# Splitting the first products of a mixture-of-experts stage, and moving the low halves of its weights behind the last gather

## The chip, the cores and the metric

The kernel runs on one core of one Trainium2 chip. The metric is the device time of the whole kernel in microseconds (us). Three runs of the kernel before took 800.58, 804.08 and 804.29 us; the median is 804.08.

## What is computed

Block-causal attention (64 tokens a block) for 8 batches, 8 heads, 576 tokens and 64 values a head. Its output, seen as 4608 tokens of 512 values, goes through a mixture of 8 experts. Each token goes to one expert, and each expert takes at most 576 tokens: the pairs of token and expert are gone through from the highest logit down, and a pair is taken if the token is still free and the expert not full.

```python
x = attn_out.transpose(0, 2, 1, 3).reshape(4608, 512)
logits = x @ w_gate
for idx in np.argsort(-logits.flatten()):
    tok, e = idx // 8, idx % 8
    if assigned[tok] >= 0 or counts[e] >= 576: continue
    assigned[tok] = e; counts[e] += 1
for e in range(8):
    mask = assigned == e
    out[mask] = np.maximum(x[mask] @ w1[e], 0.0) @ w2[e]   # w1: 512 x 1024, w2: 1024 x 512
```

Inputs and output are 32-bit floats.

## The kernel before

**The two halves of the kernel.** The attention (all lines up to the 500s) fills the first 340 us or so. It writes x to memory with each token as two 16-bit halves side by side: a high half, the value rounded to 16 bits, and a low half, what the rounding lost. The second part is the class `Moe`, and only it is touched.

**Products of halves.** The weights are split in the same way (function `weights`). A product of 32-bit accuracy is then three products of 16-bit numbers, added up in PSUM: high weight by high x, high weight by low x, low weight by high x. In `ffn` they are the list `((0,0),(0,2),(1,0))`, whose first number picks the half of the weight and whose second the half of x. Only the third reads the low half of the weight.

**Order of the work.** Nothing is written out in the order in which it is executed. Each piece of work is a Python generator that yields an engine, a cost in ns and the events that it waits for; a planner (class `Sched`) simulates the engines, always picks the piece that it believes can start first (with priorities), and only then writes its instructions. Each engine executes its own list in that order. The events are the planner's alone: on the chip an instruction waits by semaphores for the data it reads and the buffers it writes. So an event that is added or dropped changes the order of the lists, and the order decides who waits. The engines are named D (VectorE), A (ScalarE), T (TensorE), G (GpSimd, POOL in the profile) and S (SyncE, SP, which issues the plain DMAs).

**The experts one after another.** For the k-th expert in order (which expert that is comes out of the search):

- `route(k)` searches the threshold of the next expert. It begins on VectorE with a maximum over the open logits (L719), a mask (L735) and masked logits (L737), which TensorE transposes (L741). Fourteen rounds follow, in each of which VectorE (L777) and ScalarE (L750) count the logits above three candidates and TensorE adds the counts over partitions (L791, tile `tot`). The number of the expert then goes to `weights(k)`. `invert` turns the mask of chosen tokens into a list of indices; its last steps are the index products on TensorE (L915, tile `ps`) and the cast to integers on VectorE (L918, tile `ix`). L719 of the second search waits in the planner for the low half of the first expert's second row block (`('wc',0,1)`, since `GW=1`), and its transposes (L741) for the third token block (`('xm',0,2)`, `GS=2`).
- `weights(k)` loads the two matrices in eight pieces of 512 KB (SP, L966), four row blocks n = 0 to 3 of w1 and four of w2, into six `raw` buffers. For w1 of the first two experts ScalarE makes the high half with one scaling (L938) and VectorE the low half (L940, raw minus high half). All other pieces are scaled and rounded on ScalarE (L945, L949) and their low half is made on POOL (L951). A `raw` buffer is free again once its low half is made. For the first expert, the loads of w2 are held back by a one-element memset on POOL (L962) that stands behind the last gather.
- `gather(k)` fetches the chosen tokens with five indirect DMAs on POOL (L980), four of 128 tokens and one of 64 (tiles `xg`). For the first two experts `flip` transposes them on TensorE (L990, eight transposes into the PSUM tile `xt`), ScalarE copies one half (L994) and VectorE the other (L995) to the tile `X`. For later experts a DMA transposes (L1005).
- `ffn(k)` makes h (L1030) in PSUM banks shared with y, four in all (tag `g`), from 4 row blocks times 3 products. ScalarE evicts the high half with the relu (L1016, tile `HH`), VectorE the low half (L1018, `HL`). Then y for five token blocks (L1055, and L1059 for the block of 64), whose evictions (L1038, L1042) lead to the scatter on POOL (L1046). h is made in two token slices: for the first expert tokens 0 to 127 and 128 to 575, for the others 0 to 255 and 256 to 575. A slice has eight feature blocks f, taken four at a time.

For the first expert's first slice and first four feature blocks the order of the h products is by row block d: for each d all four f, so that a row block can be used as soon as it is there. Elsewhere it is by f. Both come from these two lines, and the wait in the third is for the event `wc`, set when the low half of row block d has been made:

```python
nf=4 if k==0 and h==0 and f0==0 else 1
for f,d in [(f,d) for a in range(f0,f0+4,nf) for d in range(4) for f in range(a,a+nf)]:
    yield T,3*(w/2.4+3), ... ,('wc',k,d) if k==0 else None
```

The low half of the first expert waits in the planner for its indices:

```python
yield D,1135,('ix',k),('xm',0,0) if k==0 and n in s.XC else None     # XC is empty
```

## Time and profile before

| | |
|---|---|
| median of three runs | 804.08 us (800.58 to 804.29) |
| the profiled execution | 801.86 us |
| its span, from the first to the last instruction | 800.1 us |
| mean granted TensorE clock | 0.965 |
| TensorE (PE) busy | 717.8 us, 90% of the span |
| VectorE (DVE) busy | 585.0 us, 73% |
| ScalarE (ACT) busy | 545.1 us, 68% |
| GpSimd (POOL) busy | 467.0 us, 58% |
| moved by DMA | 121.51 MB, mean 152 GB/s |
| share of PE in the chain that ended last | 58%, DVE 19%, DMA 8%, ACT 8% |

Two pieces of the profile show where the second part of the kernel lies. In the first, the span is cut in 40 slices of 20 us, and each digit is a busy share in tenths. The dip in the middle, slices 18 to 20, is the way from the last attention block through the first search to the first products:

```profile
PE   5889998899999999913898999999999999999995
PEclk9899999999999999955899999999999999999998
```

The other is the list of DMA issues; the columns are target, source, the queue, the count, the size and the median time from issue to landing. The gathers are `xg<-x,ix`:

```profile
xg<-x,ix POOLq DMA_INDIRECT x40, 4.3
out_dram<-yo,ix POOLq DMA_INDIRECT x40, 2.8
```

How the rows further down are read: a row of the timeline has the start (us from the start of the span), the length, the engine, the line of the kernel, the operation, output and inputs (with buffer numbers left out), the shape, and how many instructions it groups; in brackets stands the idle time ahead of it and what ended it. PEclk is the TensorE clock that was granted, as a share of full speed. A length is the time from the start of the first to the end of the last instruction in a row. Matmuls overlap each other in the engine, so a busy TensorE is not TensorE at its peak.

### The profile page before, as it was taken

To read this page: it belongs to the slowest core of one execution; us is meant where nothing else is said; L and a number is where in the kernel's file an instruction comes from. 1 tells how busy PE (TensorE), PEld (TensorE's weight loads), DVE (VectorE), ACT (ScalarE), POOL (GpSimd) and SP (SyncE) were. 2 spreads that over 40 slices of the span, in tenths; PEclk is the share of its full clock that TensorE was granted. 3 is DMA by queue.
4 is the path that set the end of the run, shared out by engine and by line. 5 is a ranking of instruction groups with operands and counts; after the bars stand their busy time and mean duration, and the time that the engine had idled before them with its cause. 6 is when DMAs were issued, how large, how long until landed. Compare 5 with 4: busy or idle time off the path is not lost.

```text
span 800.1 us, 19136 instructions
## 1 busy us (share of the span) xinstructions
PE 717.8 (90%) x6539; PEld 479.6 (60%) x6539; DVE 585.0 (73%) x2395; ACT 545.1 (68%) x1476; POOL 467.0 (58%) x509
## 2 busy tenths in 40 slices
PE   5889998899999999913898999999999999999995
PEld 3666676677767767601644755747557475574752
DVE  6899798988889799488787977969777683730210
ACT  5789888888988888533745859496775947392210
POOL 5788888897889876212324337475471926873001
PEclk9899999999999999955899999999999999999998
DMA  9879999999999991324408049291845819861001
GB/s 203 157 145 179 213 203 209 164 176 204 230 164 222 188 198 35 99 80 133 138 14 294 25 139 231 74 295 42 254 129 184 179 49 273 270 162 40 20 15 45
DMA packets 244305, 121.51 MB, mean 152 GB/s; under 512 B 200816, under 2 KB 227312, under 8 KB 244208
## 3 DMA queue, kind: packets, MB, share of 16 engines
q1 hardware_dynamic: 238320, 101.42, 56.1%
q0 software_dynamic: 5888, 18.88, 7.4%
q8 instruction: 51, 0.84, 0.4%
q14 instruction: 46, 0.38, 0.2%
HBM read 71.32 MB, written 18.87 MB: 113 GB/s over the span
## 4 chain that ended last, share of the span: by engine, by line
PE 58%; DVE 19%; DMA 8%; ACT 8%; issue 3%; POOL 3%; SPq 1%; POOLq 0%; DVEq 0%; ACTq 0%
PE h L1030 23%; PE y L1055 16%; PE psb L463 5%; DVE m L405 5%; PE psb L380 4%; DMA kT<-k 4%; PE psb L498 4%; ACT P L416 4%; DVE kS L350 2%; POOL P L438 2%; PE y L1059 2%; DMA xg<-x,ix 2%; ACT PT L444 2%; DVE jk L776 1%; DMA raw<-in_moe_w_dram 1%
## 5 line engine op out<-in xcount | busy, mean ns | idle before, releaser
L438 POOL TENSOR_TENSOR P<-P,m 128x320 f32<-128x320 f32 (+8 forms) x285 | 209.3, 769 | 48.2 <-DVE m L430 28.4
L1030 PE MATMUL h<-X,W 128*128 128x320 f16 (+3 forms) x1536 | 195.1, 287 | 0.0
L1030 PEld LDWEIGHTS <-W 128*128 128x128 f16 x1536 | 142.2, 98 | 42.7 <-issue 3.1
L416 ACT ACTIVATE P<-psb,m 128x576 f32<-128x576 f32 (+8 forms) x288 | 149.2, 542 | 25.8 <-DVE m L409 19.7
L1055 PE MATMUL y<-W,HH 128*128 128x512 f16 x512 | 152.2, 379 | 0.0
L951 POOL TENSOR_TENSOR W<-raw,W 128x1024 f16<-128x1024 f32 x56 | 118.4, 2136 | 40.6 <-ACT W L949 38.3
L405 DVE TENSOR_REDUCE m<-psb 128x1 f32<-128x576 f32 (+8 forms) x288 | 125.0, 481 | 12.4 <-PE psb L380 11.9
L463 PE MATMUL psb<-mident,P 128*128 128x128 f32 x800 | 106.0, 281 | 10.9 <-POOL P L438 3.6
L1046 POOL DMA_INDIRECT out_dram<-yo,ix x40 | 39.4, 986 | 113.1 <-ACT yo L1038 79.2
L380 PEld LDWEIGHTS <-qT 128*64 128x64 f16 x1408 | 78.1, 112 | 42.8 <-issue 27.8
L380 PE MATMUL psb<-kT,qT 128*64 128x288 f16 (+8 forms) x704 | 91.7, 286 | 10.2 <-ACT P L416 9.7
L463 PEld LDWEIGHTS psb<-mident,P 128*128 128x128 f32 x800 | 87.3, 142 | 22.5 <-POOL P L438 6.4
L498 PE MATMUL psb<-PT,V 128*64 128x448 f32 (+5 forms) x776 | 97.2, 388 | 2.4 <-DVE PT L446 1.9
L980 POOL DMA_INDIRECT xg<-x,ix x40 | 41.6, 1040 | 95.8 <-DVE ix L918 37.7
L1055 PE MATMUL y<-W,HL 128*128 128x512 f16 x256 | 97.0, 379 | 0.0
L1016 ACT ACTIVATE HH<-h 128x320 f16<-128x320 f32 (+3 forms) x128 | 52.1, 410 | 63.9 <-PE h L1030 59.5
L444 ACT ACTIVATE PT<-psb 128x512 f32<-128x512 f32 (+1 forms) x165 | 82.4, 592 | 5.8 <-PE psb L463 5.6
L380 PE MATMUL psb<-kS,qT 128*64 128x288 f16 (+8 forms) x704 | 84.4, 284 | 1.6 <-DVE kS L350 1.5
L1018 DVE SCALAR_TENSOR_TENSOR HL<-h,HH 128x320 f16<-128x320 f32 (+3 forms) x128 | 56.9, 452 | 38.5 <-ACT HH L1016 38.2
L1055 PEld LDWEIGHTS <-HH 128*128 128x128 f16 x512 | 46.9, 98 | 52.6 <-issue 2.0
L945 ACT ACTIVATE raw<-raw 128x512 f32<-128x512 f32 x112 | 67.4, 626 | 6.6 <-DMA raw<-in_moe_w_dram 6.5
L498 PEld LDWEIGHTS psb<-PT,V 128*64 128x64 f32 x776 | 49.5, 137 | 33.5 <-issue 24.3
(204 smaller groups left out, 1074.9 us busy)
## 6 DMA issues: line engine op xcount, KB each, us to landing
raw<-in_moe_w_dram SPq DMA_DIRECT2D x64, 512.0 KB, 5.5
x<-XR SPq DMA_DIRECT2D x8, 1152.0 KB, 5.7
kn<-in_k_dram SPq DMA_DIRECT2D x15, 576.0 KB, 5.1
qn<-in_q_dram SPq DMA_DIRECT2D x15, 576.0 KB, 7.1
V<-in_v_dram SPq DMA_DIRECT2D x64, 128.0 KB, 4.4
V<-in_v_dram SPq DMA_DIRECT2D x16, 64.0 KB, 3.9
xg<-x,ix POOLq DMA_INDIRECT x40, 4.3
out_dram<-yo,ix POOLq DMA_INDIRECT x40, 2.8
```

What stands on the lines that cost most here:

```text
L380: nc.tensor.matmul(out if len(K1.shape) == 2 else out.rearrange("p (r j) -> p r j", r=2), lhsT=A[:, h, 64 * i:64 * i + 64], rhs=K1, start= ...
L405: nc.vector.tensor_reduce(m[:, 0, c:c + 1], ps[:, o:o + 64 * (i + 1)] if g else s.part(ps, g, i, o), axis=AX.X if g else AX.XY, op=OP.max)
L416: nc.scalar.activation(out, in_, AF.Exp, bias=m[:, 1, c:c + 1], scale=s.ESC, accum_out=m[:, 2, c:c + 1])
L438: nc.gpsimd.tensor_tensor(sl, sl, m[:, 3, c:c + 1].to_broadcast([P, w]), op=OP.mult)
L444: s.nc.scalar.activation(out, in_, AF.Copy)
L463: nc.tensor.transpose(ps[:, a], s.Pb[n % s.NP][:, s.OFF[i] + 128 * j:s.OFF[i] + 128 * j + P], s.ident)
L498: nc.tensor.matmul(ps[64 * h:64 * h + 64, 64 * (i0 - b0):64 * (b1 - b0)], lhsT=vn[:, j, 2 * (n % 2) + h, :], rhs=pt[:, s.PTI[(j, i0)]:s.PT ...
L945: nc.scalar.activation(raw[:,x],raw[:,x],AF.Copy,scale=s.WS)
L951: nc.gpsimd.tensor_tensor(lw,raw,hi,op=OP.subtract)
L1018: nc.vector.scalar_tensor_tensor(HL[:,f,ts],ps,0.0,HH[:,f,ts],op0=OP.max,op1=OP.subtract)
L1030: nc.tensor.matmul(ps,lhsT=W[:,a,d,f*P:f*P+P],rhs=X[:,4*(d//2)+d%2+l,ts],start=(d==0 and n==0),stop=(d==3 and n==2))
L1055: if m<4: nc.tensor.matmul(ps,lhsT=Z[:,f,m*P:m*P+P],rhs=Y[:,a,f],start=(f==n==0),stop=(f==7 and n==2))
```

## The change

Four edits, all for the first expert (k = 0):

- the low halves of its w1 (L940) no longer wait in the planner for the index cast but for the event `gi` of the first expert, set when the last of its five gathers has been put in order on POOL. No wait on the chip is added by this; the low halves are written further back in VectorE's list. For the second expert the wait stays as it was;
- a new event `wh` is set when the high half of a row block has been put in order, and `ffn(0)` may begin with that of row block 0, where before it began with the low half;
- the first group of h products (first slice, first four feature blocks) is written as two passes: first the two products with the high half of the weights, for all four row blocks and all four feature blocks, then the product with the low half, again for all row blocks and feature blocks. The number of products is the same, and so are their inputs; only the order in which PSUM adds them up is another;
- the other h products of the first expert wait in the planner for `wc` as before.

```diff
--- before.py
+++ after.py
@@ -936,7 +936,9 @@
             if k<2 and n<4:
                 yield A,947,('wl',k,n)
                 nc.scalar.activation(hi,raw,AF.Copy,scale=s.WS)
-                yield D,1135,('ix',k),('xm',0,0) if k==0 and n in s.XC else None
+                sc.set(('wh',k,n))
+
+                yield D,1135,('ix',k) if k else ('gi',k)
                 nc.vector.scalar_tensor_tensor(lw,raw,s.WS,hi,op0=OP.mult,op1=OP.subtract)
             else:
                 for h in range(2):
@@ -1007,7 +1009,7 @@
         if m==4: sc.set(('fl',k))
     def ffn(s,k):
         nc=s.nc; fp=s.fp; sc=s.sc
-        yield S,0,('xm',k,0),('xm',k,1 if k else 0),*[('wc',k,n) for n in range(4) if k or n==0]
+        yield S,0,('xm',k,0),('xm',k,1 if k else 0),*[('wc' if k else 'wh',k,n) for n in range(4) if k or n==0]
         (W,Y),X=s.W[k],s.X[k]
         HH=fp.tile([P,8,576],F16,tag="HH",name=f"HH{k}",bufs=1); HL=fp.tile([P,8,576],F16,tag="HL",name=f"HL{k}",bufs=1)
         def hev(f,h,ps,gk,ts):
@@ -1021,15 +1023,17 @@
             w=ts.stop-ts.start
             for f0 in range(0,8,4):
                 pg={}
-                nf=4 if k==0 and h==0 and f0==0 else 1
-                for f,d in [(f,d) for a in range(f0,f0+4,nf) for d in range(4) for f in range(a,a+nf)]:
-                    yield T,3*(w/2.4+3),'g' if d==0 else None,('g2',k-1),*[('xm',k,m) for m in range(1,5) if h],('wc',k,d) if k==0 else None
-                    if d==0: gk=sc.gtake(); pg[f]=s.ps.tile([P,512],F32,tag="g",name=f"h{k}_{f}_{h}",bufs=4)[:,:w],gk
+
+                early=k==0 and h==0 and f0==0
+                for f,d,pr in [(f,d,pr) for pr in ((0,1),(2,)) for d in range(4) for f in range(4)] if early else [(f,d,(0,1,2)) for f in range(f0,f0+4) for d in range(4)]:
+                    yield T,len(pr)*(w/2.4+3),'g' if d==0 and pr[0]==0 else None,('g2',k-1),*[('xm',k,m) for m in range(1,5) if h],None if k else ('wc' if 2 in pr else 'wh',k,d)
+                    if d==0 and pr[0]==0: gk=sc.gtake(); pg[f]=s.ps.tile([P,512],F32,tag="g",name=f"h{k}_{f}_{h}",bufs=4)[:,:w],gk
                     ps,gk=pg[f]
-                    for n,(a,l) in enumerate(((0,0),(0,2),(1,0))):
+                    for n in pr:
+                        a,l=((0,0),(0,2),(1,0))[n]
                         nc.tensor.matmul(ps,lhsT=W[:,a,d,f*P:f*P+P],rhs=X[:,4*(d//2)+d%2+l,ts],start=(d==0 and n==0),stop=(d==3 and n==2))
                     sc.nolat()
-                    if d==3: sc.add(hev(f,h,ps,gk,ts),1,sc.now+200)
+                    if d==3 and 2 in pr: sc.add(hev(f,h,ps,gk,ts),1,sc.now+200)
         sca=1.0/(s.XS*s.WS*s.WS)
         def yev(m,ps,gk):
             n=P if m<4 else 64
```

In the changed kernel L940 is L942, L951 is L953, L962 is L964, L980 is L982, L990 is L992, L994 and L995 are L996 and L997, L1016 and L1018 are L1018 and L1020, L1030 is L1034, L1055 is L1059. The numbers of products, transposes and low halves are unchanged.

The order written by the planner shows the change in three places. The first is VectorE right behind the first expert's index cast (`ix0`). `W1_0` with `raw0_1024_n` is the low half of row block n, `xt0_m` the transposed token block m, `m_vm` and what follows it the beginning of the second expert's search. Before:

```order
L918 CAST ix0_5611<-ps0_5602 128x5
L940 SCALAR_TENSOR_TENSOR W1_0_5523<-raw0_1024_0_5536,W1_0_5523 128x1024
L940 SCALAR_TENSOR_TENSOR W1_0_5523<-raw0_1024_1_5541,W1_0_5523 128x1024
L719 TENSOR_REDUCE m_vm_75<-m_Lm_640 128x36
L723 MEMSET SC1_5635 128x2
L735 TENSOR_TENSOR m_nP_76<-m_Lm_640,m_vm_75 128x288
L940 SCALAR_TENSOR_TENSOR W1_0_5523<-raw0_1024_2_5545,W1_0_5523 128x1024
L737 SCALAR_TENSOR_TENSOR PV_1_5638<-m_nP_76,m_Lm_640 128x288
L995 COPY X0_5622<-xt0_0_5644 128x4x128
L940 SCALAR_TENSOR_TENSOR W1_0_5523<-raw0_1024_3_5551,W1_0_5523 128x1024
L995 COPY X0_5622<-xt0_1_5657 128x4x128
L995 COPY X0_5622<-xt0_2_5674 128x4x128
```

And after, from the first copy on:

```order
L997 COPY X0_5622<-xt0_0_5634 128x4x128
L997 COPY X0_5622<-xt0_1_5647 128x4x128
L942 SCALAR_TENSOR_TENSOR W1_0_5523<-raw0_1024_0_5536,W1_0_5523 128x1024
L997 COPY X0_5622<-xt0_2_5671 128x4x128
L997 COPY X0_5622<-xt0_3_5688 128x4x128
L942 SCALAR_TENSOR_TENSOR W1_0_5523<-raw0_1024_1_5541,W1_0_5523 128x1024
L997 COPY X0_5622<-xt0_4_5710 128x4x64
L719 TENSOR_REDUCE m_vm_75<-m_Lm_640 128x36
L723 MEMSET SC1_5750 128x2
L942 SCALAR_TENSOR_TENSOR W1_0_5523<-raw0_1024_2_5545,W1_0_5523 128x1024
L735 TENSOR_TENSOR m_nP_76<-m_Lm_640,m_vm_75 128x288
L942 SCALAR_TENSOR_TENSOR W1_0_5523<-raw0_1024_3_5551,W1_0_5523 128x1024
```

The first copy now stands directly behind the index cast and the second behind the first, ahead of all low halves; L719 stands behind two low halves as before, but also behind all five copies of X, and L737 behind all four low halves.

The second place is TensorE at the first products of all; `h0_f_0` is feature block f of the first slice, `xg0_m` a gathered token block. Before:

```order
L990 LDWEIGHTS xg0_2_5631
L990 MATMUL xt0_2_5674<-m_idh_130,xg0_2_5631 128x128
L1030 LDWEIGHTS W1_0_5523
L1030 MATMUL h0_0_0_5688<-X0_5622,W1_0_5523 128x128
L1030 LDWEIGHTS W1_0_5523
L1030 MATMUL h0_0_0_5688<-X0_5622,W1_0_5523 128x128
L1030 LDWEIGHTS W1_0_5523
L1030 MATMUL h0_0_0_5688<-X0_5622,W1_0_5523 128x128
L1030 LDWEIGHTS W1_0_5523
L1030 MATMUL h0_1_0_5695<-X0_5622,W1_0_5523 128x128
```

After:

```order
L992 LDWEIGHTS xg0_1_5626
L992 MATMUL xt0_1_5647<-m_idh_130,xg0_1_5626 128x128
L1034 LDWEIGHTS W1_0_5523
L1034 MATMUL h0_0_0_5663<-X0_5622,W1_0_5523 128x128
L1034 LDWEIGHTS W1_0_5523
L1034 MATMUL h0_0_0_5663<-X0_5622,W1_0_5523 128x128
L1034 LDWEIGHTS W1_0_5523
L1034 MATMUL h0_1_0_5666<-X0_5622,W1_0_5523 128x128
L1034 LDWEIGHTS W1_0_5523
L1034 MATMUL h0_1_0_5666<-X0_5622,W1_0_5523 128x128
L992 LDWEIGHTS xg0_2_5629
L992 MATMUL xt0_2_5671<-m_idh_130,xg0_2_5629 128x128
```

The first h products now stand behind the second token block's transposes instead of the third's, two to a feature block where there were three, and the transposes of the third block come four products later.

The third place is TensorE in the second expert's y products, around the transposes that open the search of the fourth expert (`rt3`; `y1_m` is token block m of the second expert). Before:

```order
L1055 MATMUL y1_1_7158<-W2_1_6298,HH1_6633 128x512
L1055 LDWEIGHTS HL1_6634
L1055 MATMUL y1_1_7158<-W2_1_6298,HL1_6634 128x512
L741 MATMUL rt3_7252<-mident_67,PV_3_7167 128x128 x2
L1055 LDWEIGHTS HH1_6633
L1055 MATMUL y1_1_7158<-W2_1_6298,HH1_6633 128x512
```

After:

```order
L1059 MATMUL y1_2_7242<-W2_1_6311,HH1_6591 128x512
L1059 LDWEIGHTS HL1_6592
L1059 MATMUL y1_2_7242<-W2_1_6311,HL1_6592 128x512
L741 MATMUL rt3_7265<-mident_67,PV_3_7182 128x128 x2
L1059 LDWEIGHTS HH1_6591
L1059 MATMUL y1_2_7242<-W2_1_6311,HH1_6591 128x512
```

Before, 18 of the 24 products of the second token block stand ahead of these transposes; after, all 24 and the first six of the third: 12 products more. The index products of the third expert, a little ahead of this place, moved by the same 12.

## The prediction

> **What bounds the kernel now.** I read first how busy each engine is stage by stage, then the timeline of the stage that the change touches, engine by engine, then the two later places where TensorE waits. The columns of the stage table are the stretch, and per engine the busy time and instructions, then the granted clock, the DMA share and GB/s.
>
> ```profile
> core 0: us, PE busy (x) PEld busy (x) DVE busy (x) ACT busy (x) POOL busy (x), PEclk, DMA share, GB/s
> 370.00:390.00 20.00, 13.19 (x151) 9.58 (x152) 13.85 (x49) 11.33 (x22) 7.17 (x6) 0.68 0.82 270
> 390.00:411.00 21.00, 21.00 (x151) 12.03 (x149) 19.50 (x107) 16.34 (x44) 8.50 (x4) 1.00 0.01 2
> 433.00:444.00 11.00, 7.20 (x75) 3.98 (x75) 8.12 (x36) 5.37 (x14) 4.12 (x4) 1.00 0.63 227
> 490.00:540.00 50.00, 49.94 (x383) 30.76 (x380) 40.19 (x220) 38.58 (x95) 30.97 (x21) 1.00 0.68 186
> ```
>
> From 390 on TensorE is the bound (21.00 of 21, 49.94 of 50), with one hole at 433 to 444 (7.20 of 11). So time can be won only at 370 to 390, and is lost if a new TensorE wait appears behind it. Now the gathers on POOL (start, length, idle before) and what VectorE does beside them:
>
> ```profile
> 374.07 1.18 POOL L980 DMA_INDIRECT xg<-x,ix  x1 [30.35 <-ACT W L938]
> 375.56 1.73 POOL L980 DMA_INDIRECT xg<-x,ix  x1 [0.30 <-issue]
> 377.59 1.92 POOL L980 DMA_INDIRECT xg<-x,ix  x1 [0.30 <-issue]
> 379.82 0.95 POOL L980 DMA_INDIRECT xg<-x,ix  x1 [0.30 <-issue]
> 381.07 1.27 POOL L980 DMA_INDIRECT xg<-x,ix  x1 [0.30 <-issue]
> 374.08 2.38 DVE L940 SCALAR_TENSOR_TENSOR W<-raw,W 128x1024 f16<-128x1024 f32 x2 [0.88 <-ACT W L938]
> 376.39 0.44 DVE L719 TENSOR_REDUCE m_vm<-m_Lm 128x36 f32<-128x288 f32 x1
> 377.47 1.23 DVE L940 SCALAR_TENSOR_TENSOR W<-raw,W 128x1024 f16<-128x1024 f32 x1 [0.15 <-ACT W L938]
> 380.35 1.22 DVE L940 SCALAR_TENSOR_TENSOR W<-raw,W 128x1024 f16<-128x1024 f32 x1
> ```
>
> A gather that begins while a low half (L940) runs ends 0.77 to 0.83 us after that low half does: 376.46 to 377.29, 378.70 to 379.51, 381.57 to 382.34. The fourth, already under way when the next low half begins, takes 0.95. So the low halves lengthen the second, third and fifth gathers.
>
> **The change part by part.** *Gathers.* Undisturbed ones take, in the third expert,
>
> ```profile
> 478.20 0.99 POOL L980 DMA_INDIRECT xg<-x,ix  x1 [2.70 <-DVE bs L689]
> 483.27 0.90 POOL L980 DMA_INDIRECT xg<-x,ix  x1 [0.30 <-DMA out_dram<-yo,ix]
> ```
>
> With no L940 beside them (the index cast is now followed on VectorE by copies of X, which wait for TensorE) five gathers from 374.07 take 0.99, three times 0.95 (as the fourth did above) and 0.90, with four gaps of 0.30, and end at 380.0 instead of 382.34: 2.3 us earlier. The one-element memset behind them on POOL, and the loads of the second weight matrix that SP holds for it, also come 2.3 us earlier; the third and fourth of those loads now wait for the first and second low half. These weights are needed by the first y product only at 411.00 (row further down), some 20 us after their landing, so that costs nothing in itself. One instruction that waits for it does stand in the way: on ScalarE the scaling of the third of these loads is now ahead of the first eviction of h.
>
> ```profile
> raw<-in_moe_w_dram SPq DMA_DIRECT2D x64, 512.0 KB, 5.5
> 387.90 0.28 ACT L1016 ACTIVATE HH<-h 128x128 f16<-128x128 f32 x1
> 392.32 0.28 DVE L1018 SCALAR_TENSOR_TENSOR HL<-h,HH 128x128 f16<-128x128 f32 x1
> ```
>
> By the median landing of 5.5 us that load, issued at the end of the first low half (381.65, below), is there at 387.2; the eviction is wanted at 388.6. That is 1.4 us of cover; past it each us is lost.
>
> *First products.* Rows of TensorE (and of ScalarE and VectorE for the copies of X):
>
> ```profile
> 378.72 0.62 PE L990 MATMUL xt<-m_idh,xg 128*128 128x128 f16 x8 [2.33 <-DMA xg<-x,ix]
> 379.84 1.04 PE L990 MATMUL xt<-m_idh,xg 128*128 128x128 f16 x8 [0.49 <-DMA xg<-x,ix]
> 380.91 0.60 ACT L994 ACTIVATE X<-xt 128x512 f16<-128x512 f16 x1 [0.93 <-PE xt L990]
> 381.54 0.42 DVE L995 COPY X<-xt 128x512 f16<-128x512 f16 x1
> 387.54 0.83 PE L1030 MATMUL h<-X,W 128*128 128x128 f16 x12
> 389.46 0.17 PE L791 MATMUL tot<-cn,m_bo 128*128 128x3 f16 x1 [1.09 <-ACT ja L750]
> 389.65 2.34 PE L1030 MATMUL h<-X,W 128*128 128x128 f16 x39
> ```
>
> Before, the first four feature blocks end at 388.37 and the next begin at 389.65. Now VectorE is the chain: the second token block's data land near 378.9 (its gather ends at 376.32; before it ended at 377.29 and the transposes began 2.55 later; the first block's, at 378.7, hang on the weight loads), its transposes end near 380.0, the copy at 380.45. Then low half 380.45 to 381.65; third copy, behind ScalarE's 0.60, to 382.35; fourth to 383.65, since its transposes stand behind eight products; second low half to 384.85; last copy 385.15; L719 (0.4 net) 385.55; third low half 386.75; L735 (0.4) 387.15; fourth low half 388.35; the last four products 388.6. The two evictions of 0.28 follow, so the next block begins at 389.2 to 389.6, as before. The 2.3 us of the gathers are eaten by four low halves in series: this part counts **0**, with -1.0 if the copies' waits between the low halves (1.1 us of that chain) vanish, and +0.5 if the first count of the second expert's search holds TensorE again, as the 1.09 in the row of 389.46 did.
>
> *The second expert's search starts later.* L719 waits in the planner for the low half of row block 1, and L737 now stands behind all four. In TensorE's order the transposes that open the search (L741) move from behind 15 h products to behind 48, and the index products (L915) from behind 261 products of the first expert to behind 270. Those nine are y products:
>
> ```profile
> 411.00 1.94 PE y L1055 x9
> 427.36 0.23 PE L915 MATMUL ps<-ixt,m_b 128*32 128x5 f16 x8
> 434.86 0.62 PE L990 MATMUL xt<-m_idh,xg 128*128 128x128 f16 x8 [1.75 <-DMA xg<-x,ix]
> 436.29 0.62 PE L990 MATMUL xt<-m_idh,xg 128*128 128x128 f16 x8 [0.81 <-DMA xg<-x,ix]
> 438.53 0.62 PE L990 MATMUL xt<-m_idh,xg 128*128 128x128 f16 x8 [0.97 <-DMA xg<-x,ix]
> 440.12 1.03 PE L990 MATMUL xt<-m_idh,xg 128*128 128x128 f16 x16
> 443.63 1.81 PE L1030 MATMUL h<-X,W 128*128 128x256 f16 x15
> ```
>
> So the indices come 1.94 us later (9 at 0.216), and with them the gathers and the weight loads that compete with them (SP issues these once the search has named the expert). TensorE already waits here, 1.75 + 0.81 + 0.97 = 3.5 us. Most of the delay is hidden: before, 18 y products stood behind the last transposes, ahead of the h products at 443.63; after, the order puts them ahead of the fourth block's. With landings 1.94 later, the transposes of the first four blocks begin at 436.8, 438.2, 440.45 and 442.05; six y products (0.8, an estimate: they are of two halves each) and the first six h products (0.7) follow to 444.25, and the last transposes to 444.9, against 444.35 (443.63 + 0.7) for the same work before: **+0.55**, from -0.3 (the wait for the landing shrinks) to +1.0.
>
> *The third expert's weights.* Its index products move from behind 543 products to behind 555: 12 x 0.216 = 2.6 us later against TensorE's work. On POOL the five gathers and then four low halves of 2.1 us follow:
>
> ```profile
> 487.55 6.32 POOL L951 TENSOR_TENSOR W<-raw,W 128x1024 f16<-128x1024 f32 x3
> 493.33 0.83 PE L1030 MATMUL h<-X,W 128*128 128x256 f16 x6
> 494.02 2.45 PE L1030 MATMUL h<-X,W 128*128 128x256 f16 x21
> ```
>
> The last low half ends at 493.87; TensorE reaches the product that needs it 11 products (0.11 each) after 493.33, at 494.5. So the slack is 0.65 us. POOL's list between gathers and that low half is as long as before, so it comes 0.55 + 2.6 later, at 497.0, while TensorE comes at 495.1: a wait of **+1.9**, from 0 (if the later search is paced by VectorE less than by TensorE) to +2.5. POOL has nothing to skip ahead. From the fourth expert on the index products stand six products earlier than before, and from the sixth on the order is the same, so nothing follows.
>
> *Sum.* 0 + 0.55 + 1.9 = +2.45, some +2.5 us on the profiled execution's 801.86 us, 804.4. That execution lies below the median of the three runs (804.08; 800.58 to 804.29); the mean of the four times is 802.7, and on that I put the sum: **805.2 us**.
>
> **The rivals.**
>
> *The waits are absorbed.* The planner reordered for them; if the late search catches up a round, L915 is only 0 to 1 us late, the 0.65 us of slack covers the third expert, and first part and hole cancel: about +0, 802.7. For it: the hole at 433 has 3.5 us of waiting in it that a better order can use. Against: 1.94 per nine products leaves no round to catch up, since TensorE is full.
>
> *The gain is kept.* If the first four blocks end with the data instead of with VectorE, 2.3 us are won and carried through the hole, since the search is paced by TensorE: 800.4. For it: the gathers do end 2.3 us earlier. Against: four low halves of 1.22 us after 380.
>
> *The clock drops: slower.* Rows of the clock:
>
> ```profile
> 376.00:378.00 2.00, 0.39 (x2) 0.00 (x0) 1.83 (x5) 1.06 (x1) 1.70 (x2) 0.96 0.54 180
> 378.00:380.00 2.00, 0.79 (x10) 0.62 (x11) 1.06 (x2) 1.66 (x2) 1.70 (x2) 0.89 0.48 131
> 380.00:382.00 2.00, 0.96 (x10) 0.69 (x9) 1.96 (x3) 0.60 (x1) 1.70 (x2) 0.50 0.73 168
> 386.00:388.00 2.00, 2.00 (x38) 1.91 (x36) 1.74 (x9) 1.85 (x7) 0.00 (x0) 0.90 1.05 407
> ```
>
> After a hole of 2.33 us, and 1.2 us busy in 4, the clock fell to 0.50 and came back near 386.3. In the hole at 433 (1.75 us at most at once) it stayed at 1.00. The changed kernel's waits, 2.3 us in that hole (from 434.5, where its earlier products end, to 436.8) and 1.9 us at the third expert, lie between the two. By the shares of 0.96, 0.89 and 0.90 it stood at full from 376.1 to 379.6 and at half from there to 386.4, 3.5 and 6.8 us; a spell of the shorter kind at half clock costs 1.7 us where TensorE is full. One drop: 2.5 + 1.7 = +4.2, 806.9; both: +5.9, 808.6. It decides from a wait of somewhere between 1.75 and 2.33 us, and by where the spell's boundary falls. The Trainium skill, "TensorE: Matmul & The Clock Gate", in What's actually happening and in Why this matters for your kernels, says that the clock is halved only after a whole idle window of about 3.4 us and asks for no gaps over some 3 us; by that rule neither wait would drop it and this rival would be nothing. The row of 380 to 382 speaks against the rule as it stands, so I keep the rival.
>
> **How the numbers follow.** Forecast 0.50, absorbed 0.20, gain kept 0.13, clock 0.17. The range runs from the kept gain to the double drop, 800.4 to 808.6; beyond it lie only what single runs scatter (800.58 to 804.29 here). About 0.5%, 4 us, is what a measurement of this kernel can tell from no change. Faster by more than that needs the kept gain and another 1.7 us: 0.05. Slower by more needs at least one drop: most of that rival's 0.17, less what lies under 4, 0.14. The rest, 0.81, is within 0.5%.
>
> **What would show it.** Right: five gathers of 0.90 to 1.0 us ending near 380; L942 from about 380.5 to 388.4, ending last before the first blocks; the first h products of the second feature half at 389.2 to 389.6; L915 of the second expert near 429.3, its first transposes near 436.8; and a wait of about 2 us for POOL (L953) among the first dozen h products of the third expert. Wrong: gathers still of 1.7 us or more with no low half beside them; those h products at 388 or before; no wait for L953; or a clock of 0.50 at 435 to 442 or 495 to 500.

## The result, and the profile after

The changed kernel takes 811.8 us (median of six runs, 811.31 to 816.02), the kernel before 804.18 (median of six, 800.58 to 807.52). The ratio is 1.0112, with an interval of 1.0085 to 1.0138: slower by 1.1%, some 9 us by the ratio and 7.6 by the medians, where +2.45 was forecast. The profiled execution took 811.45 us; its span is 809.7.

In that trace the first expert's index cast comes 0.92 us later than in the trace of before (373.95 against 373.03), ahead of all that was changed. So all times below are counted from the index cast of the same trace. From there to the end it is 435.7 us instead of 427.0: +8.7.

GpSimd's timeline shows the gathers, as forecast: the second to fifth take 0.91 to 0.95, and the last ends at 381.12, which is 7.17 behind the index cast, where it was 9.31.

```profile
374.98 1.18 POOL L982 DMA_INDIRECT xg<-x,ix  x1 [30.32 <-ACT W L938]
376.46 0.95 POOL L982 DMA_INDIRECT xg<-x,ix  x1 [0.30 <-issue]
...
380.21 0.91 POOL L982 DMA_INDIRECT xg<-x,ix  x1 [0.30 <-issue]
```

VectorE, TensorE and ScalarE behind them, from their timelines. The four low halves stand in a series; the last ends at 388.97, the first group at 389.42:

```profile
381.73 1.21 DVE L942 SCALAR_TENSOR_TENSOR W<-raw,W 128x1024 f16<-128x1024 f32 x1
384.54 1.22 DVE L942 SCALAR_TENSOR_TENSOR W<-raw,W 128x1024 f16<-128x1024 f32 x1
387.75 1.22 DVE L942 SCALAR_TENSOR_TENSOR W<-raw,W 128x1024 f16<-128x1024 f32 x1
```

```profile
387.52 0.40 PE L1034 MATMUL h<-X,W 128*128 128x128 f16 x4 [1.31 <-DVE W L942]
389.02 0.40 PE L1034 MATMUL h<-X,W 128*128 128x128 f16 x4 [1.11 <-DVE W L942]
390.93 2.72 PE L1034 MATMUL h<-X,W 128*128 128x128 f16 x24 [1.09 <-DVE HL L1020]
393.51 3.52 PE L1034 MATMUL h<-X,W 128*128 128x128 f16 x27
```

```profile
388.74 1.13 ACT L951 ACTIVATE W<-raw 128x512 f16<-128x512 f32 x2
389.78 0.61 ACT L947 ACTIVATE raw<-raw 128x512 f32<-128x512 f32 x1
390.30 0.59 ACT L1018 ACTIVATE HH<-h 128x128 f16<-128x128 f32 x3
```

Less the 0.92, the first group ends at 388.5 (before 388.37, forecast 388.6) and the next begins at 390.0 (before 389.65, forecast 389.2 to 389.6): the first eviction stands behind scalings and roundings of the second matrix on ScalarE (L947, L951), the last of them to 390.39. But then 27 products take 3.52 us, where 39 took 2.34 before. The stretches of 3.41 us in which the clock stands show why; the columns are those of the stage table, the stretch first, then PE busy, and PEclk as the third number from the end:

```profile
386.34:389.76 3.42, 1.13 (x10) 0.72 (x11) 3.26 (x10) 3.02 (x6) 0.27 (x1) 1.00 0.87 289
389.76:393.17 3.41, 2.31 (x23) 2.24 (x22) 2.13 (x9) 3.40 (x12) 3.11 (x2) 0.50 0.02 5
393.17:396.58 3.41, 3.41 (x32) 3.16 (x30) 2.02 (x12) 1.92 (x8) 0.88 (x1) 0.50 0.00 0
437.55:440.96 3.41, 1.22 (x9) 0.26 (x6) 2.98 (x12) 1.54 (x2) 2.80 (x3) 1.00 1.03 382
440.96:444.38 3.42, 2.96 (x22) 1.90 (x22) 0.65 (x2) 1.68 (x4) 1.28 (x2) 0.50 1.05 364
498.99:502.40 3.41, 0.00 (x0) 0.00 (x0) 2.24 (x10) 2.67 (x7) 3.41 (x3) 1.00 1.09 334
502.40:505.81 3.41, 2.98 (x15) 2.12 (x16) 1.70 (x10) 1.98 (x6) 3.21 (x3) 0.50 1.22 233
```

The clock fell to 0.50 three times: behind the stretch of the low-half products, with 1.13 us busy in it, in the hole at 438, and at the third expert. There TensorE waits 4.08 us, which it did not do before. The index cast of the third expert on VectorE, then GpSimd, SP's queue and TensorE in the changed kernel:

```profile
484.66 0.17 DVE L918 CAST ix<-ps 128x5 int32<-128x5 f32 x1 [0.72 <-PE ps L915]
```

```profile
478.43 0.99 POOL L1050 DMA_INDIRECT out_dram<-yo,ix  x1 [6.59 <-ACT yo L1042]
486.70 0.96 POOL L1050 DMA_INDIRECT out_dram<-yo,ix  x1 [7.28 <-ACT raw L947]
487.96 0.98 POOL L982 DMA_INDIRECT xg<-x,ix  x1 [0.30 <-issue]
...
493.03 0.90 POOL L982 DMA_INDIRECT xg<-x,ix  x1 [0.30 <-issue]
493.95 2.15 POOL L953 TENSOR_TENSOR W<-raw,W 128x1024 f16<-128x1024 f32 x1
...
497.31 6.29 POOL L953 TENSOR_TENSOR W<-raw,W 128x1024 f16<-128x1024 f32 x3
```

```profile
492.21 1.30 SPq L1007 DMA_TRANSPOSE X<-xg  x1
496.12 0.40 SPq L968 DMA_DIRECT2D raw<-in_moe_w_dram  x1
496.56 1.24 SPq L1007 DMA_TRANSPOSE X<-xg  x1
```

```profile
502.83 0.82 PE L1034 MATMUL h<-X,W 128*128 128x256 f16 x3 [4.08 <-DMA X<-xg]
```

A second scatter (486.70) stands ahead of the five gathers, where only one stood before. The issue of the scatter ahead of it, in the list of DMA issues for its own 0.3 us, has a landing time of 7.5 us, so it landed at 485.9; ScalarE, which the row names, had evicted the data of the second at 483.47. The gathers begin 3.3 us behind the index cast (before: 0.43). On SP the second transpose of X stands behind a load that was issued at 496.12, when the low half of 493.95 had ended and freed its buffer. Before, SP had the same order and the same wait (its low half ended at 486.34):

```profile
486.37 0.40 SPq L966 DMA_DIRECT2D raw<-in_moe_w_dram  x1
486.81 1.24 SPq L1005 DMA_TRANSPOSE X<-xg  x1
```

So what is new is where this chain starts. Counted from the second expert's first y product (467.88 before, 471.76 after), the index cast comes 3.0 later, the gathers, which also stand behind the second scatter, 5.9 later, and the second transpose of X 5.9 later. Before, that transpose landed 5.4 us after its issue, 1.07 ahead of the first h product; now it lands after 6.2, when TensorE has long been waiting.

How the +8.7 builds up, by first products (rows of the timeline, each less the index cast of its trace, the difference from before):

| from | to | forecast | measured |
|---|---|---|---|
| first index cast | first expert's first y product | 0 | +3.05 |
| there | second expert's first y product | +0.55 | -0.1 |
| there | third expert's first y product | +1.9 | +6.85 |
| there | the end | 0 | -1.1 |

### The profile page after: what moved, and what is told of

Same layout as the page of the kernel before. It is cut to its first block, busy times and chain, and to the rows that moved or that the text cites. A ratio compares the mean times of both kernels' runs of the same rounds, so it can differ in the third digit from the quotient of the medians.

```text
span 809.7 us, 19133 instructions
## 1 busy us (share of the span) xinstructions
PE 723.3 (89%) x6539; PEld 482.6 (60%) x6539; DVE 586.5 (72%) x2395; ACT 548.8 (68%) x1476; POOL 464.3 (57%) x509
## 4 chain that ended last, share of the span: by engine, by line
PE 57%; DVE 18%; DMA 9%; ACT 7%; POOL 4%; issue 3%; SPq 0%; POOLq 0%; DVEq 0%; ACTq 0%
PE h L1034 23%; PE y L1059 16%; PE psb L463 5%; DVE m L405 5%; PE psb L380 4%; DMA kT<-k 4%; PE psb L498 4%; ACT P L416 4%; PE y L1063 2%; DVE kS L350 2%; POOL P L438 2%; DMA raw<-in_moe_w_dram 2%; ACT PT L444 1%; DVE jk L776 1%; DMA out_dram<-yo,ix 1%
## 5 line engine op out<-in xcount | busy, mean ns | idle before, releaser
L1034 PE MATMUL h<-X,W 128*128 128x320 f16 (+3 forms) x1536 | 199.4, 291 | 7.9 <-DMA X<-xg 4.1
L1034 PEld LDWEIGHTS <-W 128*128 128x128 f16 x1536 | 145.0, 100 | 51.0 <-DMA X<-xg 4.2
L1059 PE MATMUL y<-W,HH 128*128 128x512 f16 x512 | 152.3, 379 | 0.0
L953 POOL TENSOR_TENSOR W<-raw,W 128x1024 f16<-128x1024 f32 x56 | 118.5, 2139 | 57.8 <-ACT W L951 57.3
L1059 PE MATMUL y<-W,HL 128*128 128x512 f16 x256 | 97.0, 379 | 0.0
L1018 ACT ACTIVATE HH<-h 128x320 f16<-128x320 f32 (+3 forms) x128 | 52.1, 409 | 65.5 <-PE h L1034 62.8
L1020 DVE SCALAR_TENSOR_TENSOR HL<-h,HH 128x320 f16<-128x320 f32 (+3 forms) x128 | 56.8, 451 | 38.9 <-ACT HH L1018 38.7
L982 POOL DMA_INDIRECT xg<-x,ix x40 | 39.1, 978 | 79.0 <-ACT W L938 30.3
L1059 PEld LDWEIGHTS <-HH 128*128 128x128 f16 x512 | 46.7, 98 | 50.8 <-issue 0.8
L947 ACT ACTIVATE raw<-raw 128x512 f32<-128x512 f32 x112 | 67.4, 623 | 9.3 <-DMA raw<-in_moe_w_dram 9.2
```

The costliest lines, as they stand in the source:

```text
L947: nc.scalar.activation(raw[:,x],raw[:,x],AF.Copy,scale=s.WS)
L953: nc.gpsimd.tensor_tensor(lw,raw,hi,op=OP.subtract)
L1020: nc.vector.scalar_tensor_tensor(HL[:,f,ts],ps,0.0,HH[:,f,ts],op0=OP.max,op1=OP.subtract)
L1034: nc.tensor.matmul(ps,lhsT=W[:,a,d,f*P:f*P+P],rhs=X[:,4*(d//2)+d%2+l,ts],start=(d==0 and n==0),stop=(d==3 and n==2))
L1059: if m<4: nc.tensor.matmul(ps,lhsT=Z[:,f,m*P:m*P+P],rhs=Y[:,a,f],start=(f==n==0),stop=(f==7 and n==2))
```

## The experiments

The runs were made in five groups, each on one chip and with runs of the kernel before beside them (medians 807.5 for e1 to e4, 803.25 for c1, c2, e5 and e6, 808.26 for e7 to e10, 803.47 for c3 and e11 to e13, 804.07 for e14 and e15); ratios are to these runs. From the fourth expert on, single traces differ by some us where the lists do not (the kernel before itself by 3.9 in c3), so I read traces only up to the third expert's first y product. This table has the place of four events against the first trace of before, counted from the first index cast. "Lag" is the third index cast less TensorE's own lateness (the second expert's first y product), "loss" what TensorE loses between the first y products of the second and third expert.

| kernel | 1st y, expert 1 | 1st y, expert 2 | 3rd index cast | lag | loss | ratio (interval) |
|---|---|---|---|---|---|---|
| after | +3.1 | +3.0 | +6.0 | 3.0 | 6.9 | 1.0112 (1.0085-1.0138) |
| c2, after again | +2.1 | +1.7 | +4.7 | 3.0 | 8.1 | 1.0116 (1.0084-1.0147) |
| e1 split only | +0.1 | +1.2 | -0.1 | -1.3 | -0.2 | 1.0017 (0.9997-1.0037) |
| e2 moved only | +0.7 | +2.0 | +5.7 | 3.6 | 8.6 | 1.0122 (1.0093-1.0151) |
| e3 scatter behind | +4.1 | +3.4 | +6.4 | 3.0 | 9.3 | 1.0129 (1.0101-1.0158) |
| e4 fill | +0.7 | +0.8 | +3.8 | 3.0 | 7.1 | 1.0084 (1.0055-1.0113) |
| e5 search free | +5.2 | +6.3 | +3.6 | -2.7 | 2.0 | 1.0093 (1.0061-1.0125) |
| e6 halves on GpSimd | +3.3 | +3.9 | +3.9 | 0.0 | 0.0 | 1.004 (1.0015-1.0065) |
| e7 before, scatter ahead | +0.3 | +0.5 | +0.5 | 0.0 | 11.1 | 1.0139 (1.0117-1.016) |
| e8 two and two | -0.3 | 0.0 | 0.0 | 0.0 | 0.3 | 1.0011 (0.9998-1.0024) |
| e9 the same, warm | +1.4 | +3.8 | +2.5 | -1.3 | -0.1 | 1.0052 (1.0032-1.0071) |
| e10 before, warm | +1.5 | +2.6 | +1.3 | -1.3 | 0.5 | 1.003 (1.0014-1.0046) |
| e11 scatters back | +2.5 | +2.7 | +5.7 | 3.0 | 6.6 | 1.0132 (1.0101-1.0164) |
| e12 the same, fill | +0.9 | +2.4 | +5.4 | 3.0 | 4.9 | 1.0129 (1.0096-1.0161) |
| e14 eight raw buffers | +2.0 | +2.3 | +5.3 | 3.0 | 6.8 | 1.0106 (1.0068-1.0143) |
| e15 before, eight | +0.7 | +0.7 | +0.7 | 0.0 | 0.0 | 0.9988 (0.9966-1.001) |

My theory when I began (A): the move of the low halves does it, by the clock behind the first group and by the scatter ahead of the third expert's gathers. Its rivals stand with each run.

**Which part of the change: e1 and e2.**

```diff
# e1, in the changed kernel
-                yield D,1135,('ix',k) if k else ('gi',k)
+                yield D,1135,('ix',k)
# e2, in the kernel before
-                yield D,1135,('ix',k),('xm',0,0) if k==0 and n in s.XC else None
+                yield D,1135,('ix',k) if k else ('gi',k)
```

> The changed kernel with the low halves back behind the index cast; the two passes of the first products stay. Numbers are the time from the first expert's index cast to the end against the kernel before (427.0 us there, 435.7 in the changed kernel, so +8.7). Theory A (the move of the low halves does it: it spaces out the second pass so that the clock falls, and makes the second search so late that a scatter gets ahead of the third expert's gathers): about 0, from -1 to +0.5; clock full from 386 on, no wait of POOL ahead of the third expert's gathers. Rival B (the two passes do it: 16 products that wait one row block at a time): +2 or more, with the clock at 0.50 around 390 to 396.

> The kernel before with its low halves moved behind the last gather; the first products in their old order, three to a row block. Theory A: the scatter stands ahead of the third expert's gathers here too, so the +5.6 of that place stays; the first group ends with the fourth low half as in the changed kernel, but each step between low halves holds twelve products instead of four, so the clock may stay: +5.5 to +9. Rival B (the two passes do it): 0 to +1.

The two passes alone change nothing that can be measured (the interval takes in 1); the move alone has the whole loss, some 10 us, a little more than was expected. That settles A against B. In e2 the clock did not fall behind the first group (twelve products to a low half instead of four), and the first y product is at +0.7 instead of +3.1. It fell in the hole and at the third expert instead.

**The clock behind the first group: e4.** Twelve products without use, in a PSUM buffer of the transposes, four (`FILL`) ahead of each of the last three row blocks:

```diff
+                    if early and 2 in pr and d and f==0:
+                        yield T,0
+                        wz=s.ps.tile([P,512],F32,tag="xt",name=f"fill{d}",bufs=2)
+                        for n in range(FILL): nc.tensor.matmul(wz,lhsT=s.ones,rhs=s.fr,start=True,stop=True)
```

> The changed kernel with twelve products more, of 512 columns and without use, four ahead of each of the second, third and fourth row block's low-half products, so that TensorE has work while it waits for the low halves. Theory A (2.7 of the +3.05 up to the first y product are the clock at 0.50 from 389.8 to 396.6): the clock stays at 1.00 there, the first y product comes 2.5 to 2.8 us earlier, +5.5 to +6.3 in all. Rival D (that part is lost to VectorE and ScalarE, which hold the evictions; the clock is a symptom): the clock stays, but the time is within 0.7 of the changed kernel's.

The same stretch behind the gathers in its trace:

```profile
385.80:389.22 3.42, 3.42 (x38) 2.42 (x38) 3.42 (x7) 2.59 (x6) 0.00 (x0) 1.00 0.99 334
389.22:392.63 3.41, 2.18 (x24) 1.43 (x22) 2.17 (x13) 3.41 (x11) 2.13 (x1) 1.00 0.31 116
```

The clock stays at 1.00, and the first y product comes at +0.7 instead of +3.1: 2.4 us of the front are the clock. The 0.7 that are left are no more than e15 shows with the order of before. By the place of that product rival D falls; the ratio, 1.0084, has an interval that overlaps with that of the changed kernel. Most of the loss is elsewhere (e4 is still some 7 us slower than the kernel before).

**The scatter: e3 and e7.**

```diff
# e3, in the changed kernel
-... ('gi',1) if k==0 and m>1 else None
+... ('gi',1) if k==0 and m>1 else ('gi',2) if k==1 and m==1 else None
# e7, in the kernel before: the third expert's first gather waits for that scatter, and
# the low halves and later scatters keep their places behind it
-            yield G,1038,('ffn',k-2),('xm',k-1,m)
+            yield G,1038,('ffn',k-2),('xm',k-1,m),('ys',1,1) if k==2 else None
```

> The changed kernel; only the second expert's second scatter is kept behind the third expert's last gather, where it stood before. Theory A: the five gathers begin 0.4 us behind the index cast instead of 3.3, TensorE's wait at the third expert falls from 5.6 to about 2.4 (index cast +6.0 against +3.0 for TensorE, less 0.65 of slack): +4.2 to +5.5 in all. Rival C (the late index cast alone paces the third expert; the scatter is only queued where POOL would wait anyway): +8 to +9.

> The kernel before, low halves and first products untouched; only the second expert's second scatter is put ahead of the third expert's gathers, as it stands in the changed kernel. Theory A (the scatter waits on GpSimd for the landing of the one before it, and the five gathers wait behind it): third index cast at the same time as before, first gather of the third expert 3 to 5 us later, TensorE waits 2 to 5 us at the third expert's first products, the clock may fall there: +2.5 to +6. Rival C (gathers this early have slack enough; it was the late index cast that cost): -0.5 to +1.

e7 is some 11 us slower than the kernel before, far over the +2.5 to +6 of A. The third index cast is on time in it, and with the scatter ahead of them the gathers come 6.8 us later:

```profile
476.79 1.25 POOL L1046 DMA_INDIRECT out_dram<-yo,ix  x1 [8.72 <-ACT yo L1038]
486.21 0.96 POOL L1046 DMA_INDIRECT out_dram<-yo,ix  x1 [8.17 <-ACT W L949]
487.48 0.98 POOL L980 DMA_INDIRECT xg<-x,ix  x1 [0.31 <-issue]
```

But the 11.1 us that TensorE loses there are not the price of the scatter. Its waits up to the first h product are none for X and none for a low half:

```profile
PE tot L791 <- DVE jk L777: 5.7, 3, 2.1
PE tot L791 <- DVE CB L779: 1.9, 1, 1.9
```

The planner put ten counts of the next search (L791) between the third index cast and the first h product on TensorE, where the kernel before and the changed kernel have six, and TensorE waits for the last of these, one round after the other. So e7 shows that a scatter there delays the gathers, and leaves open what that costs where TensorE's order stays.

e3, which takes the scatter away from the changed kernel, did not gain (some 10 us, more than A and C gave): the gathers begin 0.44 behind the index cast and the first h products of the third expert come 3.3 us earlier than in the changed kernel, as expected; then two scatters stand ahead of three low halves, and TensorE waits for each of these (1.27, 1.25 and 1.25). The loss there is 9.3. That was a side effect of the edit; the next runs were made without it.

**Both put right: e11, e12 and e13.**

```diff
# e11, in the changed kernel; e12 with the products of e4 as well
+... ('wc',2,0 if m==1 else 3) if k==1 and 0<m<3 else None
# e13: e12, and
-GW=1
+GW=-1
-                yield T,214,'rt',('xm',0,s.GS) if k==1 and s.GS>=0 else None
+                yield T,214,'rt',('wc',0,3) if k==1 else None
```

> The changed kernel with the second expert's second scatter behind the third expert's gathers and its third scatter behind the low halves that these products need, nearly as before (in the third experiment two scatters stood ahead of those low halves). If the order on GpSimd is what costs at the third expert, beside the late index cast: the first products of the third expert come at +5.3 as in that experiment, but nothing is lost behind them: the first y product of the third expert at +5 to +6, all in all +4.5 to +6.5. If the order on GpSimd is not the rest: +8 or more.

> The same with the products without use between the low halves. If clock and scatter together are the loss and each was sized rightly: the two savings add up, first y product of the first expert +0.7, first products of the third expert +2.4 to +3.3 (index cast +3.8 late, 0.65 of slack, less what TensorE is late itself), all in all +2.5 to +4.5. If something is still unnamed: +6 or more.

> The same, and the three opening steps of the second search on VectorE stand ahead of the copies of X, where VectorE waits, while its counts stay behind the four low halves. This takes 0.85 out of the series of low halves and 0.45 out of the way to the transposes of the search: the first group ends 0.8 to 1.2 earlier than in the changed kernel, so the first y product at -0.5 to +0.3, the index casts of the second and third expert about +1: -0.5 to +2 in all. If the late search stays (index cast of the third expert at +3 or more): +2.5 to +4.5.

e11 and e12 missed: 1.0132 and 1.0129, both where something unnamed was to be left. In e11 the third expert's first products start early (+4.1), and the wait appears behind them, 0.8 us for a low half and 2.6 for a count of the search (L750) on ScalarE:

```profile
PE tot L791 <- ACT ja L750: 2.6, 1, 2.6
PE tot L791 <- DVE jk L777: 0.9, 1, 0.9
PE h L1034 <- POOL W L953: 0.8, 1, 0.8
```

(columns: who waits, for whom, us in all, times, longest). What holds that count up is a scatter again:

```profile
494.59 1.01 POOL L1050 DMA_INDIRECT out_dram<-yo,ix  x1 [0.17 <-issue]
500.51 0.59 ACT L1042 ACTIVATE yo<-y 64x512 f32<-64x512 f32 x1 [2.90 <-DMA out_dram<-yo,ix]
```

The second scatter now stands behind two low halves, where the kernel before has one ahead of it. It took 5.8 us to land, and only then was one of the three buffers `yo` free for ScalarE's next eviction of y; two scalings and the count stand behind that eviction. e12 has the same wait (2.48 us on ScalarE). So neither run has the late index cast with the scatters where they were, and whether the scatter or the late cast is the larger part in the changed kernel is not shown. What is shown is that the wait moves from place to place. e12 loses 4.9 there, without a fall of the clock behind it; e11 6.6, with one spell of 3.41 us, which fits the 1.7 between them. e13 is the slowest of all, 1.0188 (1.014 to 1.0235), over all that was expected of it. The trace that there is of it shows its longest execution (824.64 us), so why it is slow stays open.

**The late search: e5 and e6.**

```diff
# e5, in the changed kernel
-GW=1
+GW=-1
# e6: e5, and for the first expert's third and fourth low half
+                    yield A,947
+                    nc.scalar.activation(raw,raw,AF.Copy,scale=s.WS)
+                    yield G,2079,('gi',k)
+                    nc.gpsimd.tensor_tensor(lw,raw,hi,op=OP.subtract)
```

> The changed kernel; only the second expert's search no longer waits in the planner for a low half, so that its first steps stand behind the index cast again, ahead of the copies of X. Theory A (what is lost behind the front is lost because the search starts late): index products of the second expert 15 products earlier than before, the gathers of the third expert no longer behind a second scatter; the two steps of the search between the low halves are gone, so the first group ends 0.8 to 1.2 earlier; the clock may still fall in its second pass. +1 to +4 in all. Rival E (the low halves themselves, wherever the search starts, cost the time): +7 to +9.

> As the one above, and the third and fourth low half are made on GpSimd right behind its gathers, after a scaling in place on ScalarE, while VectorE makes the first two. If the series of four low halves on one engine is what eats the earlier gathers, the first group ends 3 us earlier than in the changed kernel, the clock does not fall behind it, and the whole is -3 to 0 against the kernel before. If not (GpSimd and VectorE hold each other up, or ScalarE's two scalings hold the copies of X), +2 or more.

Both take away the lag at the third expert (-2.7 and 0.0), and with it the second scatter ahead of its gathers, and most of the loss there (2.0 and 0.0). So the late second search is what makes that loss; the two runs do not part the late cast from the scatter, since both go. Both pay at the front. e5 is some 7.5 us slower than the kernel before, which is what rival E gave and not A, and e6 some 3 us, which is what was expected in case its engines hold each other up. In e5 the counts of the search get between the low halves on VectorE (the last one begins 16.0 us behind the index cast instead of 13.8), and the clock is low up to 385.8 and again from 392.6 to 399.4. In e6 a low half on VectorE takes 5.01 us beside two on GpSimd, and the clock is low from 387.4 to 397.6:

```profile
382.51 5.01 DVE L948 SCALAR_TENSOR_TENSOR W<-raw,W 128x1024 f16<-128x1024 f32 x1
```

```profile
382.22 4.21 POOL L945 TENSOR_TENSOR W<-raw,W 128x1024 f16<-128x1024 f32 x2
```

**A milder move: e8.** Only the third and fourth low half behind the gathers.

```diff
-                yield D,1135,('ix',k) if k else ('gi',k)
+                yield D,1135,('ix',k) if k or n<2 else ('gi',k)
```

> The changed kernel, but with only the third and fourth low half behind the last gather; the first and second behind the index cast as before. Theory A (a series of four low halves behind the gathers is what costs, and a late search): the second gather stays long, the third and fifth become 0.95 and 0.91, gathers end 1.3 earlier than before; the search begins as before and the third expert's scatter stands as before; first group ends 1 to 2 earlier: -2 to 0. Rival F (any low half behind the last gather delays the copies of X by its 1.2 us each): +0.5 to +3.

The lag and the time are those of before: 1.0011, which is neither the gain of A nor clearly the loss of F. The gathers end 1.3 us earlier, and the first y product gains 0.3 of it.

**The clock ahead of the first products: e9 and e10.** The edit in e8 and in the kernel before:

```diff
-NWU=8
+NWU=14
```

> As the one above, with 14 instead of 8 products without use while TensorE waits for the first gather. By the shares of busy time in the traces so far (the clock falls after a 3.41 us stretch with up to 0.38 to 0.50 busy, and comes back after one with 0.79 or more) the clock does not fall near 380: 0.5 to 2.5 less than the one above. If the first group is paced by data and VectorE alone: the same as the one above.

> The kernel before with 14 instead of 8 such products, and nothing else. Clock theory: the stretch behind the first eight (0.25 busy before) is busy by 0.7 or more, so the clock stays full from 376 on and does not fall at 379.6: -0.5 to -2.5. If the first group is paced by data alone: -0.3 to +0.3; if the products without use hold up the first transposes: +0.5 to +1.

Both missed, and are slower. In e10 the clock held at 380, as the clock theory said, and then fell one stretch later:

```profile
376.30:379.70 3.40, 2.17 (x15) 0.94 (x13) 3.21 (x7) 1.75 (x3) 2.49 (x3) 1.00 0.49 163
379.70:383.10 3.40, 1.24 (x16) 0.90 (x16) 2.00 (x10) 1.15 (x3) 2.48 (x3) 1.00 0.56 154
383.10:386.50 3.40, 2.72 (x25) 2.23 (x26) 1.19 (x4) 2.16 (x7) 0.00 (x0) 0.50 0.83 294
```

At full clock the transposes that TensorE does between two gathers are shorter, so the stretch has only 1.24 us of work, and the low clock falls on the h products instead of on the transposes. The planner also put all transposes ahead of the h products.

**What the loads' waits for buffers add: e14 and e15.** Every engine's list stays as it was; only the loads wait less for buffers.

```diff
-raw=wp.tile([P,1024],F32,tag="raw", ... ,bufs=6)
+raw=wp.tile([P,1024],F32,tag="raw", ... ,bufs=8)
```

> The changed kernel with eight buffers for the raw weights instead of six; every engine's list stays word for word the same, only the waits of loads for buffers go. Theory G (the third index cast falls 3.0 us behind TensorE; less 0.65 of slack that is 2.4, and what TensorE loses there beyond it, 5 to 7 in all, comes from loads on SP that wait for buffers which GpSimd's low halves free, with the transposes of X and the scalings queued behind them): the loss at the third expert falls to 2.4 to 4.1, and +4 to +6.5 in all against the kernel before. If GpSimd's own list (scatter, five gathers, four low halves) is the whole of it: +8 to +9.

> The kernel before with eight raw buffers, lists unchanged. If waits for buffers cost something there as well (at the first products of the fourth and fifth expert): -0.5 to -3. If not: -0.3 to +0.3; if the earlier loads slow the gathers: +0.5 to +2.

In e14 SP issues the second transpose of X at 491.92, right behind its load, and no longer behind a low half; counted from the second expert's first y product that is 3.2 earlier than in the changed kernel. TensorE's waits at the third expert:

```profile
PE h L1034 <- DMA X<-xg: 1.7, 1, 1.7
PE tot L791 <- DVE jk L777: 0.9, 1, 0.9
PE h L1034 <- POOL W L953: 0.7, 1, 0.7
```

The first h products of the third expert lose 3.2 instead of 5.6, so the loads that wait for buffers are one link of the chain to X. But the clock fell for two stretches there (499.2 to 506.0) instead of one, and took the gain back: loss 6.8, time 1.0106, which is where the rival of G had it. The two h waits are 2.4 in all, the number of theory G, but not for its reason: in this run too the second scatter stands ahead of the gathers, which begin 3.2 behind the index cast, and the last of the four low halves ends 5.7 later against TensorE than before, not 3.0. The kernel before does not change (0.9988), and its trace has no lag and no loss.

**Controls: c1, c2, c3.** The two kernels once more, unedited.

> The kernel before once more, for a trace taken on the same chip as the ones beside it: 427 us from the first expert's index cast to the end, as in its first trace, or up to 4 more if this chip moves data more slowly.

> The changed kernel once more, for a ratio and a trace on the same chip as the ones beside it: 1.008 to 1.014 of the kernel before; the scatter ahead of the third expert's gathers and the low clock behind the first group again.

> The kernel before once more, for a trace on the chip of the runs beside it: 427 to 431 us from the first index cast to the end; where it is over 428, the excess lies at the first products of the fourth and fifth expert.

c1 agrees with the first trace of before within 0.3 us everywhere (the first y product at +0.2, the end at -0.2), c2 with the first trace of after in lag, loss and time. c3 took 809.24, over 5 us more than the median beside it, and 432.0 from the first index cast to the end, a little beyond what was expected: between the fourth and the fifth expert's products a scatter waited for one that landed after 9.0 us, and TensorE waited 4.1 for a count. Such a scatter may be part of what runs of one kernel differ by.

## Why the prediction was wrong, step by step

- *The gathers*: right. 0.91 to 0.95 each, the last ends at 380.2 (forecast 380.0).
- *VectorE's series and the first group*: right. Last low half at 388.05 (forecast 388.35), first group at 388.5 (388.6). The 2.3 us are eaten, as forecast.
- *The next block at 389.2 to 389.6*: too early by 0.4. The cover on ScalarE was counted for one scaling of the second matrix; a row of scalings and roundings stood there, up to 390.39.
- *"This part counts 0"*: failed, by the clock. I followed the waits of the second pass and did not add up how little TensorE works in them: 1.13 us in a stretch of 3.42. The rival of the clock looked at single holes of 1.75 to 2.33 us and at two other places. Three gaps of 0.27, 1.31 and 1.11 with four products between them do the same. It costs 2.4 of the 3.05 (e4).
- *The second expert, +0.55*: right within its bounds (-0.1), in part by luck. The index cast came 2.2 later against TensorE (5.27 - 3.05; forecast 1.94), the hole hid it, and the clock did fall in it, as that rival said; it fell mostly on transposes.
- *The third expert, +1.9*: the step that failed most, +6.85. Two terms of it held: the index cast is 3.0 late against TensorE (forecast 2.6), and "POOL's list between gathers and that low half is as long as before": from the first gather to the end of the fourth low half it takes 15.64 us, before 15.67. What failed is the way from the cast to the gathers, which the forecast took to be as short as before (0.43). It was 3.30, since a second scatter stands ahead of the gathers and starts only 0.8 behind the landing of the first. So POOL's work came 5.9 late against TensorE and not 2.6. Nor was the wait the one that I had priced: TensorE did not wait for L953 at all, but 4.08 us for X, which hangs on the same gathers and, through SP's loads, on the first low half. To the first h product 5.6 are lost. That is the 5.9, less the 1.07 that the transpose of X had to spare, plus the 0.8 that it took longer to land; e14 takes 2.4 off it. The slack of 0.65 at the last low half no run measures. The rest, behind the first product, is a fall of the clock: 1.2 in the changed kernel and 2.6 in c2 (in e14 3.6, with the 0.7 of a low half in it).
- *The scatter* ahead of the gathers was not in the prediction at all: I had compared the rows behind the gathers, not the one ahead. By the rows it is 2.9 of the 5.9. How much of the time it is stays open: e7 changes TensorE's order as well, and e3, e11 and e12 win 3.8 to 4.2 us at the first h product and lose them to other waits behind it, which their own places for the scatters bring in.
- *The rivals*: the clock's, with two drops, gave 808.6; the measured time lies 3.2 above it, since its base was too low and it had missed a third drop. "The gain is kept" and "absorbed" are refuted by the result; in e8 even a milder move keeps only 0.3 of the 1.3 us that its gathers win.

No version here beats the kernel before: e1, e8 and e15 are as fast, the others slower. Open is what e13 waits for, and how the loss at the third expert divides between the late index cast and the scatter.

## What to carry to other kernels

Work that looks harmful because it lengthens a transfer may be cheap where it stands, if its engine would only wait there: before, the low halves lay in VectorE's wait for the gathers; behind them they were four times 1.22 us in series. If a change makes an index or address late against the bound engine, do not price one wait behind it: look at what now stands ahead of it in each queue, then list every queue that hangs on it (here GpSimd, SP, ScalarE) and which buffers they hand each other. In the seven traces with a lag of 3.0 us the third expert lost 4.9 to 9.3, though none of them has the lag alone. And add up TensorE's busy time by stretches of 3.4 us, not by single gaps.

## What the runs showed of the hardware

*The clock goes by the share of busy time in a stretch.* In all these traces the granted clock changes on a grid of 3.41 us. Behind a stretch with 0.0, 1.13 or 1.22 us busy it fell from 1.00 to 0.50 (rows above); behind 1.89 it did not, in the hole of the kernel before:

```profile
434.18:437.59 3.41, 1.89 (x20) 1.16 (x20) 2.08 (x10) 1.24 (x3) 2.24 (x2) 1.00 1.03 383
```

In the changed kernel it came back behind stretches with 2.96 or more (87%) and stayed at 0.50 behind one with 2.31 (68%). The busy time alone does not draw a sharp line: the clock held behind 1.42 us in c3 (587.19) and fell behind 1.72 in e4 (378.98); it came back behind 2.71 in e3 (502.22) and stayed low behind 2.92 in e6 (387.42). The Trainium skill, "TensorE: Matmul & The Clock Gate", in What's actually happening, has the grid of 3413 ns, which agrees; that the clock is halved behind a whole idle window does not agree with the 1.13 and 1.22 us of work in the stretches that it fell behind.

*GpSimd can lock VectorE out.* A low half on VectorE (two inputs in SBUF) took 5.01 us instead of 1.22 in e6: it began 0.29 behind the start of two subtractions on GpSimd and ended 1.09 behind the end of the second. The Trainium skill, "SBUF — State Buffer", in Who interferes with whom, says that such a pair contends and that whoever comes first holds the other up for the whole instruction; the trace agrees, and shows that VectorE did not get in between the two.

*A scatter can land late, and the next waits for it.* The median in the page of before is 2.8 us from issue to landing. Beside or just behind the six loads of 512 KB of the third expert one took 7.5 in the changed kernel, and 9.0 at the same place before (474.26), where five gathers and a low half stood between it and the next scatter, which began 3.3 behind the landing. In the changed kernel, c2 and e14 the next scatter stands directly behind it and starts 0.79 behind its landing each time, with the gathers queued behind; in c3 one starts 0.3 behind a landing that took 9.0.
